# Loading ScalarE's Gelu table between two weight issues: where a table load sits in a queue that also issues DMA

## The chip, the cores and the metric

One core of one Trainium2 chip. The metric is the device time of one execution, in microseconds (us). Timed runs are compared by state: a run that is over 1.5% above the fastest of its kernel counts as slow and is left out of ratios. Where a ratio is given, it is the mean time of one kernel's fast runs over that of the other's fast runs of the same rounds, with a 95% interval; it is not quite the ratio of the medians quoted beside it. A profile is one single execution, taken by the hardware profiler; times inside it count from its first instruction.

## The reference

```python
B, S, D, F = 32, 32, 1024, 3584          # x: 1024 rows of 1024, bfloat16
def reference(x, w_gate, w_up, w_down):
    return (gelu_tanh(x @ w_gate) * (x @ w_up)) @ w_down
```

## The kernel before

Every operation is recorded with the tiles that it reads and writes; a small scheduler then gives each engine its list and puts in the semaphore waits. Each engine is given its list in a fixed order. ScalarE's list holds not only activations but also DMA issues (`dma_start` on "act"). And a wait is put in only where data demands it, so the program makes a DMA issue with no dependency wait for nothing but its place in the list.

The first product, x times w_gate and x times w_up, is built for four column tiles at once (in eight accumulator banks). The contraction dimension of 1024 is cut into eight blocks of 128. A block k needs three things: its slice of w_gate, its slice of w_up, and its slice of x transposed. Blocks 0 and 1 of x are transposed on TensorE; those from 2 up come from a transposing DMA on SyncE's queue.

```python
def load_first(eng, j, k0, k1, after=()):          # j = 0: w_gate, j = 1: w_up
    dma(eng, first[:, j, k0:k1, :], w_r[j][:, k0:k1, 0:4 * P], 0, f"w0_{j}_{k0}", after)

def load_x(h, k0, k1, after=()):
    pr.add("sp", "dma_start_transpose", xT[h][:, k0:k1, :], ...)

for k in range(NX):                                # NX = 2: blocks 0 and 1
    load_first("sp", 0, k, k + 1)
    load_first("act", 1, k, k + 1)
for k0, k1 in ((2, 3), (3, 4), (4, 5), (5, 6), (6, 8)):
    load_x(0, k0, k1)
for k in range(2, 4):                              # blocks 2 and 3, both on ScalarE
    load_first("act", 0, k, k + 1)
    load_first("act", 1, k, k + 1)
act(warm[:, 0:1], const0, GELU, 0)                 # one tiny Gelu: makes the build put the table load here
# ... cut: transposes of blocks 0 and 1 on TensorE ...
for m, j, k in steps:                              # eight matmuls for each block
    op = mm(2 * m + j, first[:, j, k, m * P:(m + 1) * P], xT[0][:, k, :], ...)
    if k == 3:                                     # partial sums of blocks 0 to 3 are evicted
        ...                                        # cut: ACT Copy or DVE copy, into `kept`
    if (m, j) == (3, 1) and k < 2:                 # blocks 4, 5 after block 0; 6, 7 after block 1
        load_first("act", 0, 2 * k + 4, 2 * k + 6, [op])
        load_first("act", 1, 2 * k + 4, 2 * k + 6)
```

(The last part is condensed.) After this start come more column tiles of the same kind, then the main part, a long sequence of fp32 matmuls.

## Time and profile before

| | before |
|---|---|
| median of 3 timed runs | 273.38 us (273.16 to 274.22) |
| the profiled execution | 976.1 us |
| TensorE busy in the profile | 99% of the span, 1182 matmuls |

The profiled execution is more than three times as long as the timed ones, so the profile has to be read with care: what ScalarE does in the first microseconds (block 3 issued at 3.24 and 3.72 us, table load at 4.22 us) is as in a later profile of the same kernel at full rate, the control below (3.25, 3.73 and 4.24 us); what TensorE does is not. From the page of the profile of before, the busy time of each engine (us, share of the span, instructions) and the chain that ended last:

```profile
PE 966.8 (99%) x1182; PEld 436.0 (45%) x1192; DVE 208.5 (21%) x237; ACT 134.8 (14%) x210; POOL 36.6 (4%) x23
...
PE 99%; issue 1%; ACT 0%
PE ps L117 99%; ACT arena L117 0%
```

TensorE is the whole chain. From the timeline of before, the weight loads of three early matmuls (start, duration, in brackets the idle time before):

```profile
2.14 0.26 PEld L117 LDWEIGHTS ps<-const-bfloat16-1.0 128*128 128x128 bf16 x1 [0.58 <-issue]
2.98 0.26 PEld L117 LDWEIGHTS ps<-const-bfloat16-1.0 128*128 128x128 bf16 x1 [0.58 <-issue]
3.82 0.26 PEld L117 LDWEIGHTS ps<-const-bfloat16-1.0 128*128 128x128 bf16 x1 [0.58 <-issue]
```

The starts are 0.84 us apart. Later profiles of this study show matmuls of the same 512 columns 0.427 or 0.216 us apart: in the profiled execution of before TensorE ran at about a quarter of the rate that goes with 0.216 us. Below, full rate means the spacing of 0.216 us, half rate that of 0.427 us. Next, the timeline of ScalarE in before ("ACTq" lines are DMA issues from its queue, "ACT" lines are work on the engine):

```profile
2.28 0.45 ACTq L117 DMA_DIRECT2D arena<-in_w_gate_dram  x1
2.76 0.45 ACTq L117 DMA_DIRECT2D arena<-in_w_up_dram  x1
3.24 0.45 ACTq L117 DMA_DIRECT2D arena<-in_w_gate_dram  x1
3.72 0.47 ACTq L117 DMA_DIRECT2D arena<-in_w_up_dram  x1
4.22 1.28 ACT L117 ACT_TABLE_LOAD   x1 [4.22 <-issue]
5.51 0.20 ACT L117 ACTIVATE warm<-const-float32-0.0 128x1 f32<-128x1 f32 x1
```

The four issues are block 2 and block 3. They start 0.48 us apart, and the table load stands behind them. Last, DMA in before, by windows of one microsecond; the last two columns are the mean busy share of the 16 DMA engines (values over 1 occur) and GB/s:

```profile
core 0: us, PE busy (x) PEld busy (x) DVE busy (x) ACT busy (x) POOL busy (x), PEclk, DMA share, GB/s
...
2.00:3.00 1.00, 1.00 (x3) 0.28 (x2) 0.00 (x0) 0.00 (x0) 0.00 (x0) 1.00 0.85 254
...
6.00:7.00 1.00, 1.00 (x8) 0.78 (x6) 0.33 (x2) 0.00 (x0) 0.00 (x0) 1.00 1.19 200
...
11.00:12.00 1.00, 1.00 (x3) 0.31 (x2) 0.00 (x0) 0.00 (x0) 0.00 (x0) 1.00 0.13 26
```

From 2 to 11 us every window of one microsecond reads 0.85 to 1.34, and the next one 0.13: DMA is saturated in this stretch, and what is issued then takes long to land. The gate weights of block 3 (128 KB), issued at 3.24 us, landed 5.4 us later; those of blocks 4 and 5 (256 KB), issued at 14.36 us, took 2.8 us. This document calls that a backlog.

### The profile page before, as it was taken

To read this page: it belongs to the slowest core of one execution; us is meant where nothing else is said; L and a number is where in the kernel's file an instruction comes from. 1 tells how busy PE (TensorE), PEld (TensorE's weight loads), DVE (VectorE), ACT (ScalarE), POOL (GpSimd) and SP (SyncE) were. 2 spreads that over 40 slices of the span, in tenths; PEclk is the share of its full clock that TensorE was granted. 3 is DMA by queue.
4 is the path that set the end of the run, shared out by engine and by line. 5 is a ranking of instruction groups with operands and counts; after the bars stand their busy time and mean duration, and the time that the engine had idled before them with its cause. 6 is when DMAs were issued, how large, how long until landed. Compare 5 with 4: busy or idle time off the path is not lost.

```text
span 976.1 us, 3280 instructions
## 1 busy us (share of the span) xinstructions
PE 966.8 (99%) x1182; PEld 436.0 (45%) x1192; DVE 208.5 (21%) x237; ACT 134.8 (14%) x210; POOL 36.6 (4%) x23
## 2 busy tenths in 40 slices
PE   9999999999999999999999999999999999999998
PEld 3222235555555555555444443442224555555554
DVE  0112222123212321231120202045000433114100
ACT  0011122111221112121111120100000000012110
POOL 0000000000000000001101010000000000000000
DMA  5530100101301003003000020400000000000000
GB/s 129 134 82 0 43 0 1 43 0 37 92 1 43 0 0 119 0 2 85 1 0 0 2 74 0 150 1 1 0 11 11 1 0 0 0 0 22 16 5 21
DMA packets 46895, 27.46 MB, mean 28 GB/s; under 512 B 8480, under 2 KB 46880, under 8 KB 46880
## 3 DMA queue, kind: packets, MB, share of 16 engines
q1 hardware_dynamic: 44656, 25.30, 9.4%
q10 hardware_dynamic: 2224, 1.97, 0.8%
q8 instruction: 9, 0.15, 0.1%
q14 instruction: 6, 0.05, 0.0%
HBM read 23.33 MB, written 2.10 MB: 26 GB/s over the span
## 4 chain that ended last, share of the span: by engine, by line
PE 99%; issue 1%; ACT 0%
PE ps L117 99%; ACT arena L117 0%
## 5 line engine op out<-in xcount | busy, mean ns | idle before, releaser
L117 PE MATMUL ps<-S,T 128*128 128x512 f32 x560 | 465.4, 1102 | 0.0
L117 PEld LDWEIGHTS ps<-S,T 128*128 128x128 f32 x560 | 240.2, 429 | 221.0 <-issue 212.7
L117 PE MATMUL ps<-T,S 128*128 128x512 f32 x224 | 185.2, 1098 | 0.0
L117 PE MATMUL ps<-arena 128*128 128x512 bf16 x186 | 155.2, 1105 | 3.4 <-issue 3.4
L117 PEld LDWEIGHTS ps<-T,S 128*128 128x128 f32 x224 | 96.0, 429 | 88.1 <-issue 88.1
L117 PEld LDWEIGHTS ps<-arena 128*128 128x128 bf16 x192 | 41.4, 221 | 113.9 <-issue 108.7
L117 PE MATMUL ps<-arena,hT 128*128 128x512 bf16 x109 | 90.2, 1106 | 1.9 <-issue 1.9
L117 ACT ACTIVATE tmp<-ps 128x512 f32<-128x512 f32 x64 | 38.1, 597 | 335.3 <-PE ps L117 335.3
L117 DVE TENSOR_TENSOR hT<-tmp,ps 128x512 bf16<-128x512 f32 x56 | 38.5, 687 | 189.9 <-PE ps L117 187.5
L117 DVE TENSOR_TENSOR tmp<-ps,tmp 128x512 f32<-128x512 f32 x28 | 19.4, 692 | 244.4 <-PE ps L117 244.4
L117 ACT ACTIVATE ps<-ps 128x512 f32<-128x512 f32 x44 | 25.6, 582 | 233.7 <-PE ps L117 233.7
L117 DVE TENSOR_TENSOR T<-arena,T 128x1024 fp32r<-128x1024 bf16 x42 | 51.0, 1220 | 29.9 <-PE ps L117 29.8
L117 POOL TENSOR_TENSOR T<-arena 128x1024 fp32r<-128x1024 bf16 x17 | 35.9, 2123 | 528.4 <-DVE T L117 499.5
L117 PEld LDWEIGHTS ps<-arena,hT 128*128 128x128 bf16 x112 | 24.5, 221 | 67.1 <-issue 66.5
L117 DVE TENSOR_TENSOR T<-arena 128x1024 fp32r<-128x1024 bf16 x25 | 30.0, 1219 | 104.6 <-PE ps L117 104.6
L117 PE MATMUL ps<-S 128*128 128x512 f32 x56 | 46.3, 1092 | 0.0
L117 PEld LDWEIGHTS ps<-S 128*128 128x128 f32 x56 | 23.9, 427 | 22.0 <-issue 22.0
L117 DVE TENSOR_TENSOR ps<-ps,tmp 128x512 f32<-128x512 f32 x32 | 22.3, 698 | 53.0 <-PE ps L117 53.0
L117 ACT ACTIVATE tmp<-tmp 128x512 f32<-128x512 f32 x28 | 17.7, 631 | 67.7 <-DVE tmp L117 67.7
L117 PE MATMUL ps<-arena,tmp 128*128 128x512 bf16 x31 | 26.1, 1100 | 0.5 <-issue 0.5
L117 ACT ACTIVATE hT<-ps 128x512 f32<-128x512 f32 x14 | 8.4, 597 | 67.8 <-PE ps L117 67.8
L117 DVE TENSOR_TENSOR S<-hT,S 128x1024 fp32r<-128x1024 bf16 x7 | 8.6, 1226 | 39.0 <-PE ps L117 39.0
(29 smaller groups left out, 112.6 us busy)
## 6 DMA issues: line engine op xcount, KB each, us to landing
arena<-in_w_down_dram SPq DMA_DIRECT2D x4, 1792.0 KB, 9.4
arena<-in_w_gate_dram SPq DMA_DIRECT2D x10, 512.0 KB, 4.1
arena<-in_w_up_dram SPq DMA_DIRECT2D x10, 512.0 KB, 5.4
out_dram<-arena SPq DMA_DIRECT2D x12, 128.0 KB, 1.7
arena<-in_w_gate_dram SPq DMA_DIRECT2D x4, 256.0 KB, 5.0
arena<-in_w_up_dram SPq DMA_DIRECT2D x4, 256.0 KB, 5.0
arena<-in_w_up_dram ACTq DMA_DIRECT2D x4, 128.0 KB, 4.7
arena<-in_w_gate_dram ACTq DMA_DIRECT2D x2, 256.0 KB, 2.8
```

The lines of the kernel that those rows point to most:

```text
L117: ins = name(eng, *args, **kw) if callable(name) else getattr(eng, name)(*args, **kw)
```

## The change

Intent: the Gelu table is needed only when the first true Gelu comes (15.78 us in the profile after), but ScalarE's queue is busy issuing. The change loads the table in the middle of the issues, not behind them.

```diff
         for k in range(2, 4):
             load_first("act", 0, k, k + 1)
             load_first("act", 1, k, k + 1)
-        act(warm[:, 0:1], const0, GELU, 0)
+            if k == 2:
+                act(warm[:, 0:1], const0, GELU, 0)
```

In the program's order only this moves: the tiny Gelu, with the table load that the build puts ahead of it, now stands ahead of the two issues of block 3. Nothing is added or removed: both profiles have 3280 instructions, 210 of them work on ScalarE.

## The prediction

> **What bounds the kernel now.** The page gives TensorE 99% of the span and the chain of waits is 99% matmuls, but this profiled execution took 976.1 us against 273.4 us timed. The timeline shows why: in the start, 512-column matmuls come 0.84 us apart (weight loads at 2.14, 2.98, 3.82), although the clock column says 1.000. [...] At a quarter of 0.84 us, 0.21 us, the 1182 matmuls come to about 250 us, so the timed kernel is also TensorE bound[...]. What delays TensorE in the start is paid in full at the end. But the profile hides the start's real waits: its slow TensorE never waits for a weight.
>
> **What the change moves.** Nothing is added or removed. On ScalarE the table load (1.283 us) and the tiny Gelu (0.203 us) move ahead of the two weight issues of block 3. [...] the Gelu follows the load at once (4.22+1.28, 5.51). Before: issues at 2.28, 2.76 (block 2), 3.24, 3.72 (block 3), table load at 4.22, Gelu until 5.71. After: table load from 3.24, Gelu until 4.75, block 3 issued at about 4.75 and 5.25: 1.5 us later.
>
> **How much is critical.** An earlier table gains nothing: ScalarE's next work waits for TensorE (idle 22.6 us here; the plan puts it near 10 us at full clock). The loss is limited by a backlog: the DMA windows show the 16 engines saturated from 2 to 11 us, and ScalarE's queue moves only 120 to 160 KB per us. Summing its packets by the microsecond, x and blocks 0 to 2 (640 KB) are through at about 6.6 us, all 896 KB at about 9. Block 3's packets, starting about 1.3 us after issue (as the first ones did), reach the queue at about 6.1, just before it would run dry. So they should land at most 0.5 us later, and the transposed x and block 2 perhaps 0.2 us sooner. TensorE at full clock would want block 3 at about 9 to 10 us, near its landing. The transposed x of block 3 lands at about the same time, and blocks 4 to 7 are requested only when TensorE has finished blocks 0 and 1, which does not move. Expected net: 0 to +0.4 us.
>
> **Prediction.** 273.6 us, range 272.8 to 274.9 (8 in 10). Faster by over 2%: 0.01; within 2%: 0.97; slower by over 2%: 0.02.
>
> **What would show it.** ScalarE's timeline: table load near 3.2, block 3 issued near 4.8 and 5.3, later work unmoved. That queue's DMA packets without a hole between 5 and 8 us. If the profile falls at full clock: TensorE's wait ahead of block 3's matmuls no more than 0.5 us longer.
>
> **What would make it wrong.** If TensorE waits for block 3 and the queue does run dry, up to 1.5 us is lost[...]. [...] If the relief to the x transposes and block 2 counts more, it gets up to 0.5 us faster.

## The result, and the profile after

| | before | after |
|---|---|---|
| median | 273.44 us (273.04 to 274.22, 6 runs) | 273.53 us (273.13 to 274.16, 6 runs) |
| ratio, 95% interval | | 1.0001, 0.9982 to 1.002 |
| profiled execution | 976.1 us | 271.1 us |

The time is the same. The profile of the changed kernel fell at full rate (512-column matmuls 0.216 us apart from 4.54 us on), so it shows the start as TensorE runs it at that rate. Its page:

```profile
PE 266.6 (98%) x1182; PEld 190.4 (70%) x1192; DVE 203.2 (75%) x237; ACT 131.9 (49%) x210; POOL 37.2 (14%) x23
...
PE 98%; issue 0%; ACT 0%; DVE 0%
```

TensorE is still the whole chain, in 271.1 us.

Its timeline of ScalarE, against the lines of before above:

```profile
2.28 0.45 ACTq L117 DMA_DIRECT2D arena<-in_w_gate_dram  x1
2.77 0.45 ACTq L117 DMA_DIRECT2D arena<-in_w_up_dram  x1
3.25 1.28 ACT L117 ACT_TABLE_LOAD   x1 [3.25 <-issue]
3.31 0.39 ACTq L117 DMA_DIRECT2D arena<-in_w_gate_dram  x1
3.73 0.47 ACTq L117 DMA_DIRECT2D arena<-in_w_up_dram  x1
4.54 0.20 ACT L117 ACTIVATE warm<-const-float32-0.0 128x1 f32<-128x1 f32 x1
```

This is the surprise. The table load runs on the engine from 3.25 to 4.53 us, and the issues of block 3, which stand behind it in the same list, go out at 3.31 and 3.73 us, during the load and even ahead of the tiny Gelu that precedes them in the list. Before, they went out at 3.24 and 3.72. So they moved by 0.07 and 0.01 us, not by 1.5 us. From the timeline of the changed kernel, the weight loads of the first blocks:

```profile
4.51 3.15 PEld L117 LDWEIGHTS ps<-arena 128*128 128x128 bf16 x16 [0.48 <-DMA arena<-in_w_gate_dram]
8.04 1.42 PEld L117 LDWEIGHTS ps<-arena 128*128 128x128 bf16 x8 [0.38 <-issue]
9.90 0.13 PEld L117 LDWEIGHTS ps<-arena 128*128 128x128 bf16 x2 [0.43 <-issue]
```

Block 2 starts at 8.04 us and block 3 at 9.90 us. The trace also records when every DMA has landed. In this profile the transposed x of block 2 landed at 7.94 us and that of block 3 at 9.79 us, just ahead of those two starts, while the gate weights of block 3 had landed at 8.62 us and the up weights, which are needed four matmuls later, at 9.58 us. Block 3 waits for x, not for the weights that the change touched.

### The profile page after: what moved, and what is told of

It reads as the page before. It is cut to its first block, busy times and chain, and to the rows that moved or that the text cites. A ratio compares the mean times of both kernels' runs of the same rounds, so it can differ in the third digit from the quotient of the medians.

```text
span 271.1 us, 3280 instructions
## 1 busy us (share of the span) xinstructions
PE 266.6 (98%) x1182; PEld 190.4 (70%) x1192; DVE 203.2 (75%) x237; ACT 131.9 (49%) x210; POOL 37.2 (14%) x23
## 4 chain that ended last, share of the span: by engine, by line
PE 98%; issue 0%; ACT 0%; DVE 0%
PE ps L117 98%; ACT arena L117 0%; DVE arena L117 0%
## 5 line engine op out<-in xcount | busy, mean ns | idle before, releaser
L117 PE MATMUL ps<-S,T 128*128 128x512 f32 x560 | 129.2, 391 | 0.0
L117 PEld LDWEIGHTS ps<-S,T 128*128 128x128 f32 x560 | 105.1, 188 | 22.4
L117 PE MATMUL ps<-T,S 128*128 128x512 f32 x224 | 51.3, 390 | 0.0
L117 PEld LDWEIGHTS ps<-T,S 128*128 128x128 f32 x224 | 42.0, 188 | 8.8
L117 PE MATMUL ps<-arena 128*128 128x512 bf16 x186 | 42.0, 379 | 0.7 <-DVE arena L117 0.3
L117 PEld LDWEIGHTS ps<-arena 128*128 128x128 bf16 x192 | 17.4, 97 | 24.3 <-issue 3.2
L117 PE MATMUL ps<-arena,hT 128*128 128x512 bf16 x109 | 24.0, 379 | 0.2
L117 PEld LDWEIGHTS ps<-arena,hT 128*128 128x128 bf16 x112 | 10.9, 98 | 13.3 <-issue 0.3
L117 DVE TENSOR_TENSOR S<-hT 128x1024 fp32r<-128x1024 bf16 x14 | 16.6, 1219 | 0.0
L117 ACT ACTIVATE T<-arena 128x1024 fp32r<-128x1024 bf16 x14 | 14.8, 1059 | 0.0
L117 PE MATMUL ps<-S 128*128 128x512 f32 x56 | 12.9, 389 | 0.0
```

The costliest lines, as they stand in the source:

```text
L117: ins = name(eng, *args, **kw) if callable(name) else getattr(eng, name)(*args, **kw)
```

## The experiments

Two theories of why nothing changed. **A, hand-over:** ScalarE's queue hands a table load to the engine and goes straight on to the DMA issues behind it, so the change moves almost nothing. **B, backlog alone:** the queue is held while the table loads, as the prediction supposed, and what saves the kernel is that late issues still land in time. They can both hold in part: A may be right of the issue, and B's backlog may be right of a delay that one forces.

The table below is the common yardstick for the experiments that were profiled at full rate. All values are read from matmul starts and DMA completions in the traces: when TensorE's matmuls first came at full rate (the recorded expectations call this the clock opening; the granted clock reads 1.00 before and after it, in the control from 2 to 16 us), when block 3 and block 4 started, when block 3's parts had landed, and the time from the start of block 4 to the start of the last matmul of the kernel.

| kernel | full rate from | x of block 3 | gate, up of block 3 | block 3 starts | block 4 starts | from there to the last matmul |
|---|---|---|---|---|---|---|
| before, as control | 6.62 | 9.96 | 8.45, 9.59 | 10.72 | 12.45 | 256.24 |
| changed | 3.71 | 9.79 | 8.62, 9.58 | 9.93 | 11.68 | 256.24 |
| changed, again | 3.65 | 10.28 | 9.15, 9.92 | 10.41 | 12.13 | 256.23 |
| load first | 5.75 | 10.49 | 9.34, 10.13 | 10.86 | 12.59 | 256.38 |
| forced wait | 6.96 | 8.48 | 8.79, 9.92 | 10.84 | 12.57 | 256.23 |
| wait, four Gelus | 3.50 | 8.02 | 9.46, 11.07 | 9.66 | 13.51 | 257.97 |
| wait, six Gelus | 6.57 | 8.28 | 10.81, 11.64 | 10.86 | 14.14 | 256.23 |
| no tiny Gelu | 5.28 | 9.89 | 8.59, 9.62 | 10.03 | 11.76 | 256.20 |

The last column is nearly one number, but for the row of the four Gelus, which is taken up there. In the other rows the rest takes 256.2 to 256.4 us once block 4 has started: what the start loses is paid in full, and nothing later takes it up. (The five looks at the queue, further below, are not in the table. Their last columns would be 256.26, 256.27, 256.32, 256.73 and 258.06; the last two lost more time behind the start of block 4.)

### The kernel before, as a control

No edit. It was run to get a profile of before at full rate.

> The kernel before, word for word, run again as a control, and in the hope of a profile at full clock. Ratio to before 1.000, 95% interval within 0.998 to 1.002. If its profile falls at full clock (matmuls of 512 columns 0.216 us apart): ScalarE issues the two weight loads of block 3 at 3.24 and 3.72 us, they land at about 8.6 and 9.8 us, the transposed x of block 3 lands at about 9.8 to 10.1 us, and TensorE starts block 3 right after that; span 271.0 to 271.7 us, as the changed kernel's 271.1.

Measured: 273.84 us median (6 runs) against 273.60 (11 runs), ratio 1.0004, interval 0.9984 to 1.0024. Its ScalarE timeline:

```profile
3.25 0.46 ACTq L117 DMA_DIRECT2D arena<-in_w_gate_dram  x1
3.73 0.47 ACTq L117 DMA_DIRECT2D arena<-in_w_up_dram  x1
4.24 1.28 ACT L117 ACT_TABLE_LOAD   x1 [4.24 <-issue]
5.53 0.20 ACT L117 ACTIVATE warm<-const-float32-0.0 128x1 f32<-128x1 f32 x1
```

Block 3's weights were issued and landed within 0.2 us of what the expectation said. TensorE did not start block 3 right after its x, though, and the span was 271.8 and not at most 271.7 us: x landed at 9.96 and block 3 started at 10.72. Its timeline of weight loads says why:

```profile
5.86 0.15 PEld L117 LDWEIGHTS ps<-arena 128*128 128x128 bf16 x1 [0.28 <-issue]
6.29 0.15 PEld L117 LDWEIGHTS ps<-arena 128*128 128x128 bf16 x1 [0.28 <-issue]
6.62 6.36 PEld L117 LDWEIGHTS ps<-arena 128*128 128x128 bf16 x30 [0.18 <-issue]
```

Until 6.6 us the matmuls of block 0 came 0.427 us apart, at half rate; from then on thirty weight loads run without a gap worth the name. In the changed kernel's first profile full rate had come at 3.71 us, and TensorE then ran into the waits for x. So the 0.7 us between the two spans (271.8 and 271.1 us) goes with the moment at which full rate sets in, and that moment varies from profile to profile (3.5 to 7.0 us over all kernels here). Whether the change has a part in it, the profiles of these two kernels cannot say: the only one of before at full rate reached it late (6.62 us), both of the changed kernel (the second follows) early (3.71 and 3.65 us). But the forced wait below loads the table just as early and reached it at 6.96 us, and the timed runs of the two kernels cover the same range.

### The changed kernel, again

No edit.

> The changed kernel once more, on one chip with the runs before it: ratio 1.000, interval within 0.998 to 1.002. Its ScalarE issues of block 3 again at 3.31 and 3.73 us, within 0.1 us of before's. If the clock of TensorE opens near 6.4 us, as in the control's profile, and not near 3.7 us, as in the first profile of the changed kernel, its block 4 starts at 12.45 us as the control's does, within 0.15 us, and the 0.7 us between the two first profiles was the moment of the clock and not the change.

Measured: 273.72 us (6 runs) against 273.59 (11 runs), ratio 1.0002, interval 0.9984 to 1.0019. Block 3 was issued at 3.31 and 3.73 us again. The test with a late full rate could not be made, because full rate set in early once more, at 3.65 us. What this profile adds: with full rate as early, block 4 started 0.45 us later than in the first profile, because the transposed x of blocks 2 and 3 landed 0.48 and 0.49 us later (8.42 and 10.28 us). That is the difference between two executions of one and the same kernel, and it is several times the 0.07 us by which the change moved an issue.

### The table load ahead of everything

```diff
         NX = 2
+        act(warm[:, 0:1], const0, GELU, 0)
         for i, eng in enumerate(("sp", "act")):     # the first issue of all: x of blocks 0 and 1
...
-        act(warm[:, 0:1], const0, GELU, 0)          # as in the kernel before, behind block 3
```

> The table load and the tiny Gelu ahead of everything that ScalarE issues. Theory A (a DMA issue does not wait for the table load or an activation ahead of it, ScalarE's queue only hands the load over in about 0.06 us): all six weight issues and the x issue slip by 0.06 to 0.15 us against the 0.74, 1.25, 1.80, 2.28 us of the changed kernel, the first x issue starts before the table load has ended, time within 0.2 us of before, ratio 0.999 to 1.001. Rival B (the queue is held while the table loads, and the changed kernel was spared for another reason): the x issue starts at 2.0 us or later, TensorE's transposes start 1.2 to 1.5 us later, time 1.2 to 1.7 us longer, ratio about 1.005.

Measured: 273.56 us (6 runs) against 273.60 (11 runs), ratio 0.9996, interval 0.9976 to 1.0017. Its ScalarE timeline:

```profile
0.73 1.28 ACT L117 ACT_TABLE_LOAD   x1 [0.73 <-PEq L590]
0.79 0.47 ACTq L117 DMA_DIRECT2D hT<-in_x_dram  x1
1.29 0.97 ACTq L117 DMA_DIRECT2D arena<-in_w_up_dram  x2
...
2.29 0.45 ACTq L117 DMA_DIRECT2D arena<-in_w_gate_dram  x1
```

The x issue starts 0.06 us behind the start of the load, long before its end at 2.01 us, and by the fourth issue (2.29 against 2.28) even that is gone. Rival B said 2.0 us or later for the first issue, and a ratio near 1.005. On this point B is refuted and A holds: this table load (0.73 to 2.01 us) did not hold the DMA issues behind it (0.79 us and on). The tiny Gelu, on the other hand, starts only after the load, at 2.03 us. In this one profile the transposed x of block 2 landed at 9.01 us, a microsecond later than in the control, and TensorE waited for it; the timed runs show no such cost, and it was not followed up.

### The delay that the prediction had supposed, forced

```diff
+            if k == 2:
+                warmed = act(warm[:, 0:1], const0, GELU, 0)
...
-            load_first("act", 0, 3, 4)
+            load_first("act", 0, 3, 4, [warmed])    # semaphore wait for the end of the tiny Gelu
```

> The changed order, with a semaphore wait that holds the first issue of block 3 until the tiny Gelu has ended: the delay that the prediction had supposed. Issues at about 4.8 and 5.2 us instead of 3.31 and 3.73. Theory A (backlog and slack): the weights land at 8.6 to 9.1 and 9.6 to 10.2 us instead of 8.62 and 9.58, block 3 still starts when its transposed x has landed (9.8 us, or up to 0.3 us sooner), time within 0.2 us of before, ratio 0.998 to 1.001. Rival B (the delay passes through to the landing): gate weights land at 10.1 us, up weights at 11.1 us, TensorE loses 0.3 to 0.6 us, ratio 1.001 to 1.002.

Measured: 273.77 us (6 runs) against 273.60 (11 runs), ratio 1.0002, interval 0.9982 to 1.0022. Its ScalarE timeline:

```profile
4.54 0.20 ACT L117 ACTIVATE warm<-const-float32-0.0 128x1 f32<-128x1 f32 x1
4.78 0.34 ACTq L117 DMA_DIRECT2D arena<-in_w_gate_dram  x1
5.15 0.46 ACTq L117 DMA_DIRECT2D arena<-in_w_up_dram  x1
```

This is the schedule of the prediction: block 3 is issued at 4.78 and 5.15 us, 1.5 and 1.4 us later. And yet its weights landed at 8.79 and 9.92 us, only 0.17 and 0.34 us later than in the changed kernel's first profile, and no later than in its second (9.15 and 9.92 us). The two lines of DMA issues in those windows, first of the changed kernel, then of this one (name, queue, count, KB each, median us from issue to landing), show the same: the time from issue to landing shrinks by 1.3 us (5.3 to 4.0 us), nearly all that the issue was late.

```profile
arena<-in_w_gate_dram ACTq DMA_DIRECT2D x1, 128.0 KB, 5.3
```

```profile
arena<-in_w_gate_dram ACTq DMA_DIRECT2D x1, 128.0 KB, 4.0
```

So the second half of the prediction stands by itself: had the issue slipped by 1.5 us, the kernel would have been as fast. Meanwhile other parts that were under way in the same stretch came sooner, and by more than the prediction's 0.2 us: the transposed x of block 3 at 8.48 instead of 9.79 us, the up weights of block 2 at 6.89 instead of 7.72 us. This did not show in the time. In the profiled execution full rate set in late (6.96 us), and block 3 started at 10.84 us, long after its x; in an execution with an early full rate it might save some 0.2 us (an estimate: in the changed kernel's first profile the gaps between matmuls ahead of blocks 2 and 3 were 0.295 and 0.348 us, where the others there were 0.216 us), which these intervals cannot see. The profile with twelve Gelus, further below, is such an execution: its full rate set in at 3.71 us and block 3 was issued at 4.77 us, its x landed at 7.86 us, and block 3 started at 9.72 instead of 9.93 us; yet the span is the changed kernel's 271.1 us.

### A long wait, as a positive control, and a middle one

```diff
+            if k == 2:
+                act(warm[:, 0:1], const0, GELU, 0)
+                for i in range(6):                  # 4 in the middle version
+                    warmed = act(S[:, i, :], one, GELU, 0)
...
+            load_first("act", 0, 3, 4, [warmed])    # waits for the last of them
```

The Gelus write to a buffer that is overwritten later, so results stay correct.

> A positive control: six Gelus of 128x512 behind the tiny one, and block 3's first issue waits for the last of them by semaphore. Issues at about 8 and 8.5 us, landings 10.5 to 11.5 and 11 to 12.5 us. If TensorE in the start is paid in full at the end: it waits 0.7 to 1.7 us ahead of block 3, blocks 4 and 5, whose loads queue behind, slip as well, by 1 to 2 us, and the time grows by 1 to 2.5 us, ratio 1.004 to 1.009. If there is slack later that takes it up: ratio below 1.002.

Measured with six: 274.96 us (6 runs) against 273.60 (11 runs), ratio 1.0051, interval 1.0032 to 1.007. This is half a per cent, but the interval lies clear of 1. Block 3 was issued at 7.88 and 8.28 us and landed at 10.81 and 11.64 us. The time is as expected, the place is not: TensorE lost only 0.19 us ahead of block 3 (0.403 us between two matmuls, against 0.216 us at full rate), and 1.55 us ahead of block 4, whose gate weights stand behind block 3's in the same queue, were issued at 8.80 instead of 7.47 us and landed at 14.10 instead of 11.39 us. The timeline of weight loads shows this second wait (its 1.88 us is the time in which no weight was loaded):

```profile
14.14 0.55 PEld L117 LDWEIGHTS ps<-arena 128*128 128x128 bf16 x4 [1.88 <-DMA arena<-in_w_gate_dram]
```

Block 4 started 1.69 us later than in the control, where full rate had set in at nearly the same time (6.62 us, here 6.57), and the last matmul also started 1.69 us later: the start is paid in full.

> As the long wait, with four Gelus instead of six: block 3 issued at about 6.9 and 7.3 us, 3.6 us later than the changed kernel, landing at 9.5 to 10.3 and 10.2 to 11.2 us. Block 4's issue hardly moves (about 7.8 instead of 7.5 us). With slack as the traces show it (TensorE comes to block 3 at 9.9 to 10.7 us, to its up part 0.65 to 0.86 us later): time 0 to 0.6 us over before, ratio 1.000 to 1.002. If a delay of the issue were paid in proportion (1.36 us for 4.6 us): 1.06 us, ratio 1.004.

Measured with four: 275.30 us (273.96 to 278.12, 6 runs, one of them slow; the five fast ones have a median of 274.83) against 273.59 (11 runs), ratio 1.0063, interval 1.0032 to 1.0093. This missed: 0 to 0.6 us was expected, and the median of the fast runs is up by 1.24 us, about as much as with six Gelus (1.36 us; the two intervals overlap). Block 3's issues (6.84 and 7.21 us) and landings (9.46 and 11.07 us) were nearly as written. The error lay behind them. Block 4's issue came at 7.70 us, as written, but the control, from which its 7.5 us had been taken, had reached full rate late (6.62 us). In this execution full rate had set in early (3.5 us), and the two profiles of the changed kernel, with an early full rate as well (3.71 and 3.65 us), issued block 4 at 6.46 and 6.54 us. So it was 1.2 us late, behind block 3's delayed issues in the queue. Its gate weights landed at 13.46 us, after 5.8 us, and not at 11.64 and 11.68 us, after 5.2 and 5.1 us. That block 3's packets, put off, now stood ahead of them fits the order of the queue but was not tested. TensorE stood still for 0.59 us at the up weights of block 3 and for 1.52 us at block 4. Then this happened, in windows of this profile (TensorE's busy time, its granted clock, DMA share, GB/s):

```profile
10.50:13.50 3.00, 1.23 (x5) 1.00 1.14 240
13.50:17.00 3.50, 3.27 (x8) 0.53 1.16 317
17.00:20.00 3.00, 3.00 (x15) 0.98 1.20 290
```

From 13.5 to 17 us TensorE ran at half rate (matmuls 0.427 us apart, a granted clock of 0.53), and the rest of the kernel took 257.97 us and not 256.2. So, in this profile, a spell of half rate followed the two stalls, on top of their own length; whether they caused it was not shown. (The look with twenty Gelus, below, has a mean granted clock of 0.994, too.) With six Gelus the profiled execution, with its stall of 1.55 us, kept a granted clock of 1.00. A difference in the clock may also be what spreads the runs of the middle version over 4 us: the granted clock is 0.994 for the profiled run (276.88 us), 0.992 for the slow one (278.12 us) and 1.000 for the other four. But only this one was profiled.

Together: here 1.5 us of delay was free (ratio 1.0002), 3.5 us was not (1.0063). Where between the two the slack ends was not tried.

### The tiny Gelu taken away

```diff
-            if k == 2:
-                act(warm[:, 0:1], const0, GELU, 0)
```

> The tiny Gelu taken away. The build then puts two table loads in the stream, one ahead of the first eviction by Copy (which starts near 10.3 to 11.2 us) and one ahead of the first true Gelu near 16 us. If only a load in front of waiting work costs: the first eviction on ScalarE starts 1.3 us later if the load stands behind the wait for TensorE, TensorE waits some 0.8 to 1.3 us more at block 4, whose banks the evictions free, the second load costs TensorE 0 to 1.3 us at the first banks reused; time 0.8 to 2.5 us over before, ratio 1.003 to 1.009. If the queue runs ahead and loads the table in idle time, before its wait: the first load costs nothing, and the time grows by under 0.5 us or by the second load's share alone.

Measured: 273.39 us (6 runs) against 273.59 (11 runs), ratio 0.9999, interval 0.9984 to 1.0015. The build now puts two loads in the list, one ahead of the first Copy and one ahead of the first true Gelu. Its ScalarE timeline:

```profile
9.43 1.28 ACT L117 ACT_TABLE_LOAD   x1 [9.43 <-PE ps L117]
10.72 2.06 ACT L117 ACTIVATE hT<-ps 128x512 f32<-128x512 f32 x4
12.81 1.28 ACT L117 ACT_TABLE_LOAD   x1
15.84 0.60 ACT L117 ACTIVATE tmp<-ps 128x512 f32<-128x512 f32 x1 [1.75 <-PE ps L117]
```

The loads start as soon as the work ahead of them has been issued or ended (9.43 us behind the last issue, 12.81 us behind the last eviction), in time in which ScalarE had almost nothing to do. (The first load's "<-PE" is the wait of the DMA issues ahead of it: the profile's reader puts it on the next instruction that counts as busy.) The semaphore wait belongs to the activation behind the load (15.84 us), and the load (12.81 us) did not wait with it. The second expectation holds. The first load ends at 10.71 us and the eviction follows at once. That is 0.69 us behind the start of block 3, against 0.41 us in the changed kernel, so the load held the eviction up by some 0.3 us (an estimate from these two); TensorE did not feel it, and block 4 started at 11.76 us, right in the range of the other profiles. So the place of the table load was worth nothing to begin with: the warming itself can be left out of this kernel without a measurable loss.

### How much can stand between a table load and a DMA issue

If the queue hands work over and goes on, how far does it run ahead? Full Gelus of 128x512 were put between the tiny Gelu and block 3's issues, without any wait.

```diff
+            if k == 2:
+                act(warm[:, 0:1], const0, GELU, 0)
+                for i in range(12):                 # 1, 3, 6 and 20 in the other versions
+                    act(S[:, i, :], one, GELU, 0)
```

> Twelve Gelus of 128x512 (0.518 us from start to start) behind the table load and the tiny Gelu, ahead of block 3's issues, and no wait. Theory A (the queue of ScalarE hands work over and runs ahead, a few instructions deep): the first issue of block 3 stands at 5.7 to 7.2 us, while Gelus ahead of it have still to run, well before the twelfth ends at about 10.9 us[...]. If there were no limit: 4.1 us. Rival B (an issue waits for the engine's work ahead of it): 10.9 us or later, and some 4 us of time lost. Time under A: 0 to 0.8 us over before, ratio 1.000 to 1.003.

Measured: 273.31 us (6 runs) against 273.59 (11 runs), ratio 0.9998, interval 0.9983 to 1.0013. Block 3 was issued at 4.77 us, when the first of the twelve had just started:

```profile
4.65 0.61 ACT L117 ACTIVATE S<-const-bfloat16-1.0 128x512 fp32r<-128x512 bf16 x1
4.77 0.35 ACTq L117 DMA_DIRECT2D arena<-in_w_gate_dram  x1
```

This is neither the 5.7 to 7.2 us of theory A, whose depth of a few instructions was a guess that no earlier run had shown, nor the 4.1 us without a limit, and far from rival B's 10.9 us. Twelve extra Gelus, 6.2 us of ScalarE's time, were free. The other four were single looks, so their state is unknown; the kernel before, run once beside them, took 273.90 us (twenty and six) and 274.02 us (three and one).

> One look: twenty Gelus instead of twelve ahead of block 3's issues, no wait. With twelve, the issue came at 4.77 us, which two readings give. Limit: about twelve instructions can be outstanding, so with twenty the issue comes when the ninth Gelu starts, 8.8 to 9.0 us. Pace: there is no limit in reach, and the queue takes about 0.12 us to hand over one instruction, so the issue comes at 5.6 to 6.0 us.

Measured: one run, 279.02 us; the issue came at 8.93 us, when the ninth of the twenty had just started:

```profile
4.65 4.76 ACT L117 ACTIVATE S<-const-bfloat16-1.0 128x512 fp32r<-128x512 bf16 x9
8.93 0.34 ACTq L117 DMA_DIRECT2D arena<-in_w_gate_dram  x1
```

The reading with a limit fits (8.8 to 9.0 us), and the pace (5.6 to 6.0 us) is refuted: the issue went out when eleven Gelus were left that had not started. With twelve it was the same count.

> One look: six Gelus. Limit: all six fit, so the issue comes at the pace of the hand-over alone, about 0.06 us each, 3.7 to 3.8 us. Pace of 0.12 us: 4.0 to 4.2 us.

Measured: one run, 274.46 us; issue at 4.57 us, just as the table load had ended (4.53 us). Both readings missed: behind the running table load seven activations (the tiny Gelu and six) held the issue until the load had ended.

> One look: three Gelus. If one activation behind the load is the limit: 4.55 to 4.6 us. If a count between two and seven decides: 3.4 to 3.7 us, or 4.55 if the count is below four.

> One look: one Gelu of 128x512 between the tiny Gelu and block 3's issues. With none the issue came at 3.31 us, while the table load ran; with six at 4.57 us, as the load ended. If the table load lets only one activation be handed over behind it: issue at 4.55 to 4.6 us here too. If a count of instructions decides: issue at 3.3 to 3.6 us.

Measured, one run each: with three Gelus 273.79 us and the issue at 4.55 us, with one 273.35 us and the issue at 3.34 us. The ScalarE timeline with three:

```profile
4.54 0.20 ACT L117 ACTIVATE warm<-const-float32-0.0 128x1 f32<-128x1 f32 x1
4.55 0.33 ACTq L117 DMA_DIRECT2D arena<-in_w_gate_dram  x1
```

and with one:

```profile
3.25 1.28 ACT L117 ACT_TABLE_LOAD   x1 [3.25 <-issue]
3.34 0.36 ACTq L117 DMA_DIRECT2D arena<-in_w_gate_dram  x1
```

Of the two readings for one Gelu, the count fits. Behind the running table load two activations (the tiny Gelu and one more) left the DMA issue free (3.34 us, the load from 3.25 to 4.53 us); four held it until the load had ended (4.55 us). Three were not tried. The change has one activation between the load and the issues, and its issue went out free (3.31 us). Why fewer passed behind the table load than the eleven unstarted Gelus behind running ones is open.

## Why the prediction was right or wrong

- **The time** was right: 273.6 us against 273.53 us, "within 2%" with a chance of 0.97.
- **What bounds the kernel** was right, and stronger than argued. The prediction went by the spacing of the matmuls (0.84 us) although the clock column said 1.000, took it for a quarter rate (its own estimate), and the next profile showed 0.216 us for the 0.21 us that it had worked out. "What delays TensorE in the start is paid in full at the end" is shown by the constant 256.2 us behind block 4 and by the 1.69 us of the long wait.
- **"An earlier table gains nothing"** was right: ScalarE's next work started at 10.34 us in the changed kernel, and even two loads left to the last moment cost nothing.
- **The step that failed** is "block 3 issued at about 4.75 and 5.25: 1.5 us later". Measured: 3.31 and 3.73 us, 0.07 and 0.01 us later. The prediction had added the engine's time (1.283 + 0.203 us) to the queue's time. The trace of before could have warned: it charges issues to the queue and the load to the engine, as separate lines. What it could not show is whether the two overlap, because there every issue stood ahead of the load or waited for TensorE long after it. The number came out right in spite of this step, because nothing moved that could have cost time. As far as this step goes that is luck; that it would also have come out right had the issue slipped is the merit of the next step.
- **The backlog** was right: forced by a semaphore, the same delay moved the landings by 0.17 and 0.34 us ("at most 0.5 us"), and the time not at all.
- **The relief of x and block 2** was mis-sized: 0.2 us was written, 0.8 us (up weights of block 2) and 1.3 us (x of block 3) were measured in the forced version. It brought nothing that these runs can see. (Each is one profile, and two profiles of the changed kernel differ by 0.5 us in the x of block 3.)
- **Block 3's needs** were half right: its x "lands at about the same time" as its weights, the prediction said. In the changed kernel's profile x landed 1.17 us after the gate weights and 0.21 us after the up weights, so x and not the weights set the start.
- **The load itself** took 1.283 us in both profiles, as the prediction had it from the first, and nothing more was seen behind it: in the changed kernel the load ran from 3.25 to 4.53 us and the tiny Gelu started at 4.54 us.

## What to carry to other kernels

Ask of every instruction whether it takes time on the engine or on the queue: in ScalarE's list here, a DMA issue behind a table load and one or two activations went out 0.06 or 0.09 us after the load's start (3.31 and 3.34 us, against 3.25); behind the load and four activations it came at the load's end (4.55 us), behind a semaphore wait for the tiny Gelu at 4.78 us. Before paying attention to the place of a table load, look whether the engine has idle time ahead of its first real use. And when an issue does slip inside a saturated stretch of DMA, look at the landing and at what stands behind it in the same queue, not at the issue: 1.5 us of slip cost nothing here, and 3.5 us hurt the next block (1.52 us) more than its own (0.59 us).
